# Block means of the value rows in a fused attention and MLP kernel: which operand is stationary in the matmuls that form them

## The chip, the cores and the metric

The kernel runs on one core of one Trainium2 chip. The metric is the device time of one execution in microseconds (us), as a median over runs. One execution was also taken with the hardware profiler, and all rows below are from that one.

## The reference, cut to what matters

Two batches of attention (8 heads, 768 positions, head size 64) feed two MLPs. Each query sees 31 neighbours at most and, beside them, 24 blocks of 32 positions, each standing in with the largest of its keys and the mean of its values:

```python
k_sum = k.reshape(B, H, nb, block, D).max(axis=3)
v_sum = v.reshape(B, H, nb, block, D).mean(axis=3)
...
scores_all = np.concatenate([scores_l_m, scores_s], axis=-1)
scores_all = scores_all - np.max(scores_all, axis=-1, keepdims=True)
a = np.exp(scores_all)
a = a / (np.sum(a, axis=-1, keepdims=True) + 1e-09)
v_all = np.concatenate([v, v_sum], axis=2)
return np.matmul(a, v_all).astype(np.float32)
...
h = x @ w_in
g = np.maximum(h, 0.0) + np.log1p(np.exp(-np.abs(h)))
x = g @ w_out
...
return ((x @ w1) * (x @ w2) @ w3) @ w_out2
```

The change touches only `v_sum`: a 24 x 512 table of means for each of the two batches (512 is 8 heads of 64).

## The kernel before, in words

**Attention.** The 1536 query rows are worked in 12 tiles `u` of 128, six for each batch `b`. Scores: `att_a` (L389, steps `A{u}0`, `A{u}1`) into PSUM pool `px`, tag "x". Softmax: `att_max` on DVE (L400), `att_exp` on ACT (L406), `att_inv` on DVE (L412, L413), `att_norm` on POOL (L418). Then `att_c1` turns the weights by identity matmuls into pool `pa`, tag "a" (L426, steps `T{u}0`, `T{u}1`), DVE and ACT copy them out (L435, L433), and `att_d1` multiplies with the value window `vw` (L447, step `AV{u}`) into pool `ph`, tag "h". Each value window has 96 local rows and, below them in partitions 96 to 119, the 24 means.

**The means.** `v_load` (L340) brings all 768 value rows of a batch into `vt`, 128 rows in each of six groups. `v_sum` (L347, steps `vs{b}s0` and `vs{b}s1`, three groups each) multiplies them with a table of 1/32 and zeros: `sel_t[:, a]` (128 x 24) is the stationary operand, the 512 value columns move, and six float32 matmuls add up in one bank `vs_p`. For tiles 0 and 1 the means go from `vs_p` straight into `vw` (`v0_out`, ACT L357 and DVE L359). For the others ACT copies them to SBUF (`v_keep`, L350), SP stores them to DRAM (`v_store`, L353), and `vw_sum` (L378) loads them into each window. `vs_p` of batch 0 takes a buffer of "x", that of batch 1 one of "a".

**The MLPs.** After the attention come matmuls in three float32r passes each through `mm3` (L239): `H`, `X`, `wm`, `AB`, then the products (L691) and `O`. Weights are loaded by SP (L248) and split by ACT, DVE and POOL (L259 to L283); the first of these lie in the last third of the attention.

**What sets the order.** Nothing is scheduled at run time: class `Order` writes one instruction list. A walk over the PE steps (`pe`, `COST`) gives each a due time, the other engines' steps get theirs backwards from these, and a simulation takes, for each engine, the step with the earliest due time among those that can start within a short look-ahead. Buffers of one tag are handed out strictly in the order of due times: a step whose turn in its tag has not come is not placed, even if a buffer is free. The walk has floors: tile `u` doesn't begin before `16.0 + SP1 * min(u, 8) + SP2 * max(u - 8, 0)`. The PE list goes A0, A1, `vs0s0`, `vs0s1`, then for each `u`: A of tile u+2, at `u == 3` also `vs1s0`, `vs1s1`, then T and AV of tile u. On the chip every engine and the SP queue run their lists strictly in order.

Of the kernel before, what the change touches and what calls it, by code (L numbers as in the profile page):

```python
# [8 lines left out]
F32 = mybir.dt.float32  # L9
# [14 lines left out]
class Order:  # L24
# [21 lines left out]
    def add(self, name, eng, cost, place, fn, needs=(), take=(), give=(), port=False, table=None, lead=0.0):  # L46
        assert name not in self.steps, name
        self.steps[name] = (eng, cost, place, fn, list(dict.fromkeys(d for d in needs if d)), list(take))
        self.extra[name] = (port or eng == "POOL", table, lead)
        for t, b in take:  # L50
            assert b not in self.owner, b
            self.owner[b] = t
        for b in give:
            self.users.setdefault(b, {})[name] = 1
# [150 lines left out]
def fused_kernel(ctx, tc, q, k, kwin, v, vb, w_in, w_out, w1, w2, w3, wo2, mask, sel, ident, out):  # L205
    nc = tc.nc
    P = 128
    B, NT, _, NP, _, _ = q.shape
    S = v.shape[1]
    D = 512  # L210
    NBK = 24
    W = 96
    NK = W + NBK
# [12 lines left out]
    ph = ctx.enter_context(tc.tile_pool(name="ph", bufs=2, space=bass.MemoryType.PSUM))  # L226
    px = ctx.enter_context(tc.tile_pool(name="px", bufs=4, space=bass.MemoryType.PSUM))
    pa = ctx.enter_context(tc.tile_pool(name="pa", bufs=2, space=bass.MemoryType.PSUM))
# [58 lines left out]
    ap_ = att_ctx.enter_context(tc.tile_pool(name="att", bufs=1))  # L287
    mask_t = ap_.tile([P, 3, NK], F32, name="mask_t")
    id_t = ap_.tile([P, P], F32, name="id_t")
    sel_t = ap_.tile([P, 6, NBK], F32, name="sel_t")  # L290
    vs_s = ap_.tile([P, B, D], F32, name="vs_s")

    kt = {}
    kw = {}
# [2 lines left out]
    vw = {}  # L297
# [17 lines left out]
    def kw_copy(t, eng):  # L315
        kw[t] = ap_.tile([P, 2, NP, NK], F32, tag="kw", bufs=3, name="kw")
        for blk in range(2):
            w = wins(t)[blk]
            for h in range(2):
                a, b = max(w, HALF * h), min(w + W, HALF * h + HALF)  # L320
                if a < b:
                    d, s = kw[t][:, blk, :, a - w:b - w], kt[t // NT, h][:, :, a - HALF * h:b - HALF * h]
                    if eng == "ACT":
                        nc.scalar.copy(d, s)
                    else:
                        EN[eng].tensor_copy(d, s)

    def kw_sum(t):
        nc.vector.tensor_copy(
            kw[t][:, :, :, W:NK], ks[t // NT].unsqueeze(1).to_broadcast([P, 2, NP, NBK]))  # L330

    vt = {}
    vs_p = {}

    def v_load(b, i):
        if i == 0:
            vt[b] = xt_p.tile([P, 6, D], F32, tag="xt", name="vt")
        nc.sync.dma_start(vt[b][:, 3 * i:3 * i + 3], v[b, 384 * i:384 * i + 384].rearrange("(a p) c -> p a c", p=P))  # L340

    def v_sum(b, i):
        if i == 0:
            pool, tag = ((px, "x"), (pa, "a"))[b]
            vs_p[b] = pool.tile([P, D], F32, tag=tag, name="vs_p")
        for a in range(3 * i, 3 * i + 3):
            nc.tensor.matmul(vs_p[b][W:NK], sel_t[:, a], vt[b][:, a], start=a == 0, stop=a == 5)  # L347

    def v_keep(b):
        nc.scalar.copy(vs_s[W:NK, b], vs_p[b][W:NK])  # L350

    def v_store(b):
        nc.sync.dma_start(vs_d[b], vs_s[W:NK, b])  # L353
# [8 lines left out]
    def q_load(t):  # L362
        qt[t] = ap_.tile([P, NP, 64, 2], F32, tag="q", bufs=3, name="qt")
        nc.sync.dma_start(qt[t], q[t // NT, t % NT])

    def wins(t):
        j = 2 * (t % NT)
        return [min(max(64 * i - 16, 0), S - W) for i in (j, j + 1)]
# [105 lines left out]
    def step(n):  # L474

        return n // 12, n % 12 // 4, 4 * (n // 12) + n % 4
# [256 lines left out]
    T = B * NT  # L733
# [3 lines left out]
    add = o.add  # L737
# [1 line left out]
    EN = {"POOL": nc.gpsimd, "DVE": nc.vector}  # L739


    COST = {"A": 1.0, "T": .55, "AV": 1.2, "H": 2.72, "X": 1.36, "wm": 2.72, "AB": 2.72, "O": .68, "vs": 1.3, "PR": 1.36}
    at_ = {}
    clock = [8.0]

    def pe(kind, name):
        at_[name] = clock[0]
        clock[0] += COST[kind]

    def tile_a(u):  # L750
        for h in range(2):
            pe("A", f"A{u}{h}")

    def tile_b(u):
        for h in range(2):
            pe("T", f"T{u}{h}")
        pe("AV", f"AV{u}")
# [4 lines left out]
    tile_a(1)  # L762
    for i in range(2):
        pe("vs", f"vs0s{i}")
    for u in range(T):
        clock[0] = max(clock[0], 16.0 + SP1 * min(u, 8) + SP2 * max(u - 8, 0))
        if u + 2 < T:
            tile_a(u + 2)
        if u == 3:
            for i in range(2):  # L770
                pe("vs", f"vs1s{i}")
        tile_b(u)
    pe("H", "H0")
    pe("H", "H4")
# [49 lines left out]
    def padd(kind, name, fn, needs=(), take=(), give=()):  # L824
        add(name, "PE", COST[kind], at_[name], fn, needs, take, give)

# [19 lines left out]
    for b in range(B):  # L846
        for i in range(2):
            add(f"vl{b}{i}", "SP", 3.0, None, lambda b=b, i=i: v_load(b, i), (i and f"vl{b}0",), () if i else [("xt", f"vt{b}")], lead=1)
            padd("vs", f"vs{b}s{i}", lambda b=b, i=i: v_sum(b, i), (f"vl{b}0", f"vl{b}{i}", "sell", i and f"vs{b}s0"),
                 () if i else [("xa"[b], f"vsp{b}")], (f"vt{b}",))  # L850
        add(f"vsc{b}", "ACT", .6, None, lambda b=b: v_keep(b), (f"vs{b}s1",), (), (f"vsp{b}",))
        add(f"vss{b}", "SP", .2, None, lambda b=b: v_store(b), (f"vsc{b}",))


# [27 lines left out]
    for j in jobs:  # L882
        kind, i, p = j
# [14 lines left out]
    for u in range(T):  # L898
        b = u // NT
        eng = "ACT" if u < 2 else "POOL"  # L900
        hs = [h for h in range(2) if wins(u)[0] < HALF * h + HALF and wins(u)[1] + W > HALF * h]
        add(f"kw{u}", eng, 1.3, None, lambda u=u, eng=eng: kw_copy(u, eng),
            [f"kl{2*b+h}" for h in hs], [("kw", f"kw{u}")], [f"kt{2*b+h}" for h in hs])
        add(f"q{u}", "SP", 1.0, -7.5 if u == 0 else None, lambda u=u: q_load(u), (), [("q", f"q{u}")], lead=2)
        add(f"vw{u}", "SP", 1.5, None, lambda u=u: vw_load(u), (), [("g", f"vw{u}")], lead=2)
        add(f"ks{u}", "DVE", .3, None, lambda u=u: kw_sum(u), (f"kw{u}", f"km{2*b+1}"), port=True)
        if u < 2:
            for h in range(2):
                add(f"vs{u}_{h}", "ACT" if h else "DVE", .68, None, lambda u=u, h=h: v0_out(u, h),
                    (f"vw{u}", "vs0s1"), (), ("vsp0",))  # L910
        else:
            add(f"vs{u}", "SP", .27, None, lambda u=u: vw_sum(u), (f"vw{u}", f"vss{b}"), lead=1)
        for h in range(2):
            padd("A", f"A{u}{h}", lambda u=u, h=h: att_a(u, h),
                 (f"ks{u}", f"q{u}", h and f"A{u}0"), [("x", f"sc{u}_{h}")], (f"kw{u}", f"q{u}"))
            for e in range(4 * h, 4 * h + 4):
                add(f"max{u}{e}", "DVE", .205, None, lambda u=u, e=e: att_max(u, e),
                    (f"A{u}{h}", "ml", e and f"max{u}{e-1}"), () if e else [("s", f"s{u}")], (f"sc{u}_{h}",))
                add(f"exp{u}{e}", "ACT", .39, None, lambda u=u, e=e: att_exp(u, e), (f"max{u}{e}",), table="exp")
            add(f"norm{u}{h}", "POOL", 1.0, None, lambda u=u, h=h: att_norm(u, h), (f"inv{u}",), lead=.5)  # L920
            padd("T", f"T{u}{h}", lambda u=u, h=h: att_c1(u, h), (f"norm{u}{h}", "il"),
                 [("a", f"tr{u}{h}")], (f"s{u}",))
            add(f"at{u}{h}", "ACT" if h else "DVE", .66, None, lambda u=u, h=h: att_c2(u, h), (f"T{u}{h}",),
                [("tmp", f"at{u}{h}")], (f"tr{u}{h}",))
        add(f"inv{u}", "DVE", .33, None, lambda u=u: att_inv(u), [f"exp{u}{e}" for e in range(8)])
        padd("AV", f"AV{u}", lambda u=u: att_d1(u),
             (f"at{u}0", f"at{u}1") + ((f"vs{u}_0", f"vs{u}_1") if u < 2 else (f"vs{u}",)),
             [("x" if u >= T - 3 else "h", f"av{u}")], (f"at{u}0", f"at{u}1", f"vw{u}"))
        add(f"xh{u}", "ACT", .6, None, lambda u=u: att_hi(u), (f"AV{u}", u % 4 and f"xh{u-1}"),
            () if u % 4 else [("xt", f"xt{u//4}")])  # L930
        add(f"xl{u}", "DVE", .7, None, lambda u=u: att_lo(u), (f"xh{u}",), (), (f"av{u}",))
# [11 lines left out]
    for n in range(N1):  # L943
        g, c, i = step(n)
# [13 lines left out]
    for s_ in range(12):  # L958
        g, c = divmod(s_, 3)
# [43 lines left out]
    A = lambda *rs: sorted({f"acc{r//3}" for r in rs})  # L1003
# [14 lines left out]
    for i in range(8):  # L1018
# [31 lines left out]
        for c in (1, 2):  # L1050
# [6 lines left out]
            pool = "g" if c == 1 or i == 0 else "b"  # L1057
# [6 lines left out]
    for n in range(N2):  # L1064
        c, i = divmod(n, 8)
# [84 lines left out]
```

## Time and profile before

| | us |
|---|---|
| median of 3 runs | 576.05 (575.16 to 578.75) |
| the profiled execution's own time | 574.96 |
| its span in the trace | 573.2 |

The span is the stretch from the first to the last instruction in the trace; 1.76 us of the profiled execution's time lie around it. PE is TensorE's matmuls, PEld its weight loads, DVE VectorE, ACT ScalarE, POOL GpSimd, SPq the queue of SyncE that issues the DMAs. A float32 matmul of the program stands in the trace as two matmul records with a weight load each, a transpose or a float32r matmul as one; "x12" behind a piece of the chain counts records. The granted clock is TensorE's, as a share of 2.4 GHz.

### The profile page before, as it was taken

What the parts mean: (1) busy time and instruction counts of PE and PEld (TensorE: products, weight loads), DVE (VectorE), ACT (ScalarE), POOL (GpSimd) and SP (SyncE); (2) the same over time, 40 slices, a digit from 0 to 9 for tenths busy, and PEclk for the clock granted to TensorE, in tenths of its full rate; (3) what the DMA queues carried; (4) which work ended last, traced back from release to release, by engine and by line L of the source; (5) the groups of instructions that cost most, each with busy time, mean ns of one, the idle gap of its engine ahead of it and who ended that gap; (6) DMA issues with size and microseconds to landing.
All of it is one profiled execution on the core that took longest, in us unless ns stands there. A gap on an engine that the chain in (4) does not pass through costs nothing.

```text
span 573.2 us, 8418 instructions
## 1 busy us (share of the span) xinstructions
PE 560.9 (98%) x3068; PEld 455.3 (79%) x3068; DVE 401.7 (70%) x786; ACT 322.3 (56%) x688; POOL 156.6 (27%) x143
## 2 busy tenths in 40 slices
PE   8999799999999999999999999999999999999997
PEld 4558678888888888888888888888888888888885
DVE  4668778657787586856586555675777799989710
ACT  4769976667787666665665656566654233222310
POOL 2546543022442342302230333234653000000000
PEclk9999879999999999999999999999999999999999
DMA  8897644143543453423341422225410010000021
GB/s 319 246 273 210 194 122 137 37 111 117 176 132 126 124 170 111 147 73 111 110 119 52 160 74 72 95 93 148 147 37 1 3 73 0 1 0 1 1 93 55
DMA packets 21946, 61.20 MB, mean 107 GB/s; under 512 B 2304, under 2 KB 2688, under 8 KB 21904
## 3 DMA queue, kind: packets, MB, share of 16 engines
q1 hardware_dynamic: 21904, 60.66, 34.3%
q8 instruction: 24, 0.39, 0.3%
q14 instruction: 18, 0.15, 0.1%
HBM read 55.31 MB, written 5.34 MB: 106 GB/s over the span
## 4 chain that ended last, share of the span: by engine, by line
PE 92%; DMA 3%; ACT 2%; DVE 1%; SPq 1%; POOL 0%; issue 0%; POOLq 0%
PE hps L239 23%; PE xps L239 23%; PE abps L691 13%; PE ops L239 11%; PE wps L239 8%; PE abps L239 8%; PE vs_p L347 2%; PE sc L389 2%; PE av L447 2%; DMA sel_t<-in_sel_dram 2%; PE tr L426 1%; DMA raw<-in_w_in_dram 1%; ACT s L406 1%; POOL s L418 0%; DVE vw L359 0%
## 5 line engine op out<-in xcount | busy, mean ns | idle before, releaser
L283 POOL TENSOR_TENSOR w<-cv,w 128x512 fp32r<-128x512 f32 x72 | 96.7, 1347 | 228.8 <-ACT w L279 218.1
L239 PE MATMUL hps<-xt,w 128*128 128x512 f32 x576 | 138.8, 390 | 0.0
L239 PE MATMUL xps<-gt,w 128*128 128x512 f32 x576 | 137.9, 389 | 0.0
L239 PEld LDWEIGHTS hps<-xt,w 128*128 128x128 f32 x576 | 108.4, 188 | 22.6
L239 PEld LDWEIGHTS xps<-gt,w 128*128 128x128 f32 x576 | 108.1, 188 | 22.5
L492 DVE SCALAR_TENSOR_TENSOR tm<-tm,hps 128x512 f32<-128x512 f32 x48 | 33.0, 687 | 59.3 <-ACT tm L489 59.2
L239 PE MATMUL ops<-w,pt 128*128 128x512 f32 x288 | 67.6, 389 | 0.0
L275 DVE SCALAR_TENSOR_TENSOR cv<-cv,raw 128x512 int32<-128x512 int32 x72 | 58.9, 819 | 9.3 <-ACT cv L269 7.4
L489 ACT ACTIVATE tm<-hps 128x512 f32<-128x512 f32 x48 | 28.6, 597 | 62.6 <-PE hps L239 62.6
L239 PEld LDWEIGHTS ops<-w,pt 128*128 128x128 f32 x288 | 54.1, 188 | 11.2
L263 DVE SCALAR_TENSOR_TENSOR raw<-raw 128x512 int32<-128x512 int32 x72 | 57.9, 804 | 4.8 <-ACT raw L259 4.8
L279 ACT CAST w<-cv 128x512 fp32r<-128x512 f32 x72 | 44.4, 619 | 14.2 <-DVE cv L275 9.2
L259 ACT ACTIVATE raw<-raw 128x512 int32<-128x512 uint16 x72 | 48.0, 668 | 1.7 <-DMA raw<-in_w_dram 1.7
L239 PE MATMUL wps<-w 128*128 128x512 f32 x192 | 46.1, 389 | 0.0
L239 PE MATMUL abps<-x2t,w 128*128 128x512 f32 x192 | 44.5, 389 | 0.0
L269 ACT ACTIVATE cv<-raw 128x512 f32<-128x512 f32 x64 | 42.2, 660 | 0.0
L239 PEld LDWEIGHTS abps<-x2t,w 128*128 128x128 f32 x192 | 36.0, 188 | 7.5
L239 PEld LDWEIGHTS wps<-w 128*128 128x128 f32 x192 | 36.0, 188 | 7.5
L498 DVE SCALAR_TENSOR_TENSOR hps<-hps,tm 128x512 f32<-128x512 f32 x48 | 33.5, 697 | 9.7 <-ACT tm L495 7.8
L406 ACT ACTIVATE s<-s,sm 128x120 f32<-128x120 f32 x96 | 36.6, 385 | 5.0 <-DVE sm L400 4.9
L505 DVE TENSOR_TENSOR gt<-hps,gt 128x512 fp32r<-128x512 f32 x48 | 33.0, 688 | 8.8 <-ACT gt L502 7.9
L502 ACT CAST gt<-hps 128x512 fp32r<-128x512 f32 x48 | 28.2, 588 | 15.5 <-DVE hps L498 15.5
(81 smaller groups left out, 689.2 us busy)
## 6 DMA issues: line engine op xcount, KB each, us to landing
raw<-in_w_dram SPq DMA_DIRECT2D x32, 512.0 KB, 3.5
raw<-in_w_in_dram SPq DMA_DIRECT2D x16, 512.0 KB, 3.5
raw<-in_w_out_dram SPq DMA_DIRECT2D x16, 512.0 KB, 3.5
vw<-in_v_dram SPq DMA_DIRECT2D x12, 384.0 KB, 6.5
raw<-in_wo_dram SPq DMA_DIRECT2D x8, 512.0 KB, 3.6
kt<-in_k_dram SPq DMA_DIRECT2D x4, 768.0 KB, 10.3
qt<-in_q_dram SPq DMA_DIRECT2D x12, 256.0 KB, 7.0
vt<-in_v_dram SPq DMA_DIRECT2D x4, 768.0 KB
```

The lines of the kernel that those rows point to most:

```text
L239: nc.tensor.matmul(ps, lhs(a), rhs(b), start=first and i == 0, stop=last and i == 2)
L259: nc.scalar.activation(r[:, :, 0], r.bitcast(U16)[:, :, 1], AF.Copy, bias=-(0.5 - 2.0 ** -14), scale=2.0 ** -13)
L263: nc.vector.scalar_tensor_tensor(r[:, :, 0], r[:, :, 1], -0x80000000, r[:, :, 0], ALU.bitwise_and, ALU.bitwise_or)
L269: nc.scalar.activation(f(c), h, AF.Copy, scale=2.0 ** -112)
L275: nc.vector.scalar_tensor_tensor(c, c, 3, r[:, :, 0], ALU.logical_shift_left, ALU.bitwise_or)
L279: nc.scalar.copy(w[:, 0], f(cvs[kind, i]))
L283: eng.tensor_tensor(w[:, 1], f(cvs[kind, i]), f(w[:, 0]), ALU.subtract)
L406: nc.scalar.activation(s[:, e], s[:, e], AF.Exp, bias=sm[:, 0, e:e + 1], scale=-1.0, accum_out=sm[:, 1, e:e + 1])
L492: nc.vector.scalar_tensor_tensor(tm[n], tm[n], -2.0, hps[n], ALU.mult, ALU.add)
L498: nc.vector.scalar_tensor_tensor(hps[n], hps[n], 0.0, tm[n], ALU.max, ALU.add)
L505: nc.vector.tensor_tensor(gt[n][:, 1], hps[n], f(gt[n][:, 0]), ALU.subtract)
L691: nc.tensor.matmul(ps, w[:, a, (o + kk) * P:(o + kk + 1) * P], rhs(b), start=kk == 0 and n == 0, stop=kk == 1 and n == 2)
```

## The change

`v_sum` takes the values as the stationary operand: for each of the six groups and each of four chunks of 128 columns, `vt[:, a, chunk]` (128 x 128) is loaded as weights and the four columns of `sel_t` that belong to this group move. The result `vs_t` is the table of means turned round (128 columns of the values in the partitions, 4 x 24 in the free dimension), in a buffer of "h". A new ACT step `vsT{b}` copies it to SBUF, and a new PE step `vsu{b}` turns it back into `vs_p` by four matmuls against the identity, which now also wait for the load of `id_t` (step `il`). Everything from `vs_p` on is as before.

```diff
+    vsT = ap_.tile([P, B, 4, NBK], F32, name="vsT")
...
     def v_sum(b, i):
         if i == 0:
-            pool, tag = ((px, "x"), (pa, "a"))[b]
-            vs_p[b] = pool.tile([P, D], F32, tag=tag, name="vs_p")
+            vs_t[b] = ph.tile([P, 4, NBK], F32, tag="h", name="vs_t")
         for a in range(3 * i, 3 * i + 3):
-            nc.tensor.matmul(vs_p[b][W:NK], sel_t[:, a], vt[b][:, a], start=a == 0, stop=a == 5)
+            for c in range(4):
+                nc.tensor.matmul(vs_t[b][:, c, 4 * a:4 * a + 4], vt[b][:, a, c * P:(c + 1) * P],
+                                 sel_t[:, a, 4 * a:4 * a + 4], start=True, stop=True)
+
+    def v_turn(b):
+        nc.scalar.copy(vsT[:, b], vs_t[b])
+
+    def v_back(b):
+        pool, tag = ((px, "x"), (pa, "a"))[b]
+        vs_p[b] = pool.tile([P, D], F32, tag=tag, name="vs_p")
+        for c in range(4):
+            nc.tensor.matmul(vs_p[b][W:NK, c * P:(c + 1) * P], vsT[:, b, c], id_t, start=True, stop=True)
...
-    COST = {"A": 1.0, "T": .55, "AV": 1.2, "H": 2.72, "X": 1.36, "wm": 2.72, "AB": 2.72, "O": .68, "vs": 1.3, "PR": 1.36}
+    COST = {"A": 1.0, "T": .55, "AV": 1.2, "H": 2.72, "X": 1.36, "wm": 2.72, "AB": 2.72, "O": .68, "vs": 1.2, "vsu": .55, "PR": 1.36}
...
         pe("vs", f"vs0s{i}")
+    pe("vsu", "vsu0")
...
                 pe("vs", f"vs1s{i}")
+            pe("vsu", "vsu1")
...
-                 () if i else [("xa"[b], f"vsp{b}")], (f"vt{b}",))
-        add(f"vsc{b}", "ACT", .6, None, lambda b=b: v_keep(b), (f"vs{b}s1",), (), (f"vsp{b}",))
+                 () if i else [("h", f"vst{b}")], (f"vt{b}",))
+        add(f"vsT{b}", "ACT", .3, None, lambda b=b: v_turn(b), (f"vs{b}s0", f"vs{b}s1"), (), (f"vst{b}",))
+        padd("vsu", f"vsu{b}", lambda b=b: v_back(b), (f"vsT{b}", "il"), [("xa"[b], f"vsp{b}")])
+        add(f"vsc{b}", "ACT", .6, None, lambda b=b: v_keep(b), (f"vsu{b}",), (), (f"vsp{b}",))
...
-                    (f"vw{u}", "vs0s1"), (), ("vsp0",))
+                    (f"vw{u}", "vsu0"), (), ("vsp0",))
```

## Rows read from the trace of the kernel before

**Rows 1.** Page, part 1: busy us, share of the span and instructions by engine.

```profile
PE 560.9 (98%) x3068; PEld 455.3 (79%) x3068; DVE 401.7 (70%) x786; ACT 322.3 (56%) x688; POOL 156.6 (27%) x143
```

**Rows 2.** Windows: us, busy of PE, PEld, DVE, ACT, POOL, granted clock, DMA share, GB/s.

```profile
110.00:376.00 266.00, 266.00 (x1175) 220.28 (x1174) 181.47 (x266) 172.47 (x300) 77.94 (x58) 1.00 0.36 113
```

**Rows 3.** The chain that ended last, in order of time: start, us, what.

```profile
13.53 5.32 PE vs_p L347 x12
...
18.87 0.59 ACT vw L357
...
23.80 1.15 PE av L447 x32
...
31.81 1.08 PE av L447 x32
...
33.86 5.27 PE vs_p L347 x12
39.16 0.59 ACT vs_s L350
39.74 0.14 issue
...
48.41 1.02 PE tr L426 x8
...
52.50 0.35 SPq L364
...
54.17 7.29 DMA raw<-in_w_in_dram
61.48 0.43 DVE cv L271
...
62.87 6.17 ACT s L406 x32
...
73.90 1.98 PE av L447 x32
75.88 1.89 PE tr L426 x8
...
82.01 8.43 PE hps L239 x36
...
569.38 0.69 DVE osb L725
```

**Rows 4.** Weight loads by line: duration ns min/median/max; the last from part 5: mean.

```profile
L347 PEld LDWEIGHTS vs_p<-vt,sel_t x24: 98/103/103, 13.5 to 38.1; 128*24 128x24 f32 x24
...
L447 PEld LDWEIGHTS av<-at,vw x384: 132/138/232, 23.8 to 81.7; 120*64 120x64 f32 x192
...
L426 PEld LDWEIGHTS tr<-id_t,s x96: 133/138/223, 20.6 to 77.1; 128*120 128x120 f32 x96
...
L239 PEld LDWEIGHTS hps<-xt,w 128*128 128x128 f32 x576 | 108.4, 188 | 22.6
```

**Rows 5.** Page, part 5: ACT's exponentials; busy us, mean ns, idle before.

```profile
L406 ACT ACTIVATE s<-s,sm 128x120 f32<-128x120 f32 x96 | 36.6, 385 | 5.0 <-DVE sm L400 4.9
```

**Rows 6.** SP's waits up to 82 us: total us, times, longest.

```profile
SPq L353 <- ACT vs_s L350: 6.3, 1, 6.3
```

**Rows 7.** Windows of the attention, columns as in rows 2.

```profile
22.00:24.00 2.00, 0.82 (x20) 0.60 (x16) 1.97 (x15) 2.00 (x10) 0.00 (x0) 1.00 0.52 150
...
40.00:42.00 2.00, 1.23 (x14) 0.85 (x15) 0.94 (x4) 1.71 (x8) 0.00 (x0) 1.00 1.08 239
...
64.00:66.00 2.00, 1.31 (x18) 0.88 (x14) 1.79 (x18) 2.00 (x13) 1.66 (x2) 1.00 1.00 289
66.00:68.00 2.00, 0.68 (x5) 0.41 (x4) 1.42 (x10) 2.00 (x11) 0.36 (x2) 1.00 0.46 178
68.00:70.00 2.00, 1.57 (x24) 1.39 (x26) 1.20 (x3) 2.00 (x9) 1.84 (x2) 0.55 0.00 0
...
78.00:80.00 2.00, 2.00 (x9) 1.64 (x8) 1.50 (x3) 1.93 (x4) 1.01 (x1) 0.89 0.65 240
```

More of the change, by code (lines that the diff above doesn't have):

```diff
@@ L334, in fused_kernel @@
     vt = {}
+    vs_t = {}
     vs_p = {}
```

## The prediction

> **What bounds the kernel now.** I began with the page's busy shares: PE is busy for 560.9 of 573.2 us [rows 1], so a saving elsewhere counts only where PE waits for it. The windows then show where PE is the limit for certain: from 110 to 376 us it has no idle at all [rows 2], and in the chain of waits every piece from 82.01 us to the last copy out at 569.38 is PE's [rows 3]. Everything from there on costs the same in both kernels, so the change counts by how much it moves the end of the attention, which now hands over at about 82 us.
>
> The chain of that part, in order of time [rows 3], is where the reader should look next. Both batches' means stand on it: 5.32 us at 13.53 and 5.27 us at 33.86. Behind the first come the copies by ACT and DVE into the first two windows, then PE is the chain from 23.80 to 52.50, with the second batch's means inside. At 52.50 it passes to the SP queue, to a load of weights (7.29 us to landing), to DVE, which stands at L271 until that load is in at 61.48, to the last exponentials on ACT (6.17 us), to POOL, and back to PE. So a change of PE's time before 52.50 shifts the rest, but the rest has its own sources, the transfers above all.
>
> **The matmuls of the means.** Before, a batch takes 12 records of 512 moving columns, 5.32/12 = 443 ns each [rows 3]; the weight load (24 columns) hides behind them. After, it takes 6 groups x 4 chunks = 24 matmuls, 48 records, each with a load of 128 columns, and 4 columns moving. The moving side is next to nothing: what paces a record is now the load, which no long matmul hides.
>
> No row has such a stream, so I bound it. The durations of loads grow with their columns: 98 to 103 ns for 24, 132 to 138 for 64, 188 for 128 [rows 4]. From 24 to 128 columns that is about 87 ns for 104 columns, 0.84 ns a column, so 107 ns for 128, and some 80 ns that don't depend on the columns. Whether those 80 overlap is told by `av`: 32 records in 1.08 us [rows 3] are 34 ns each over two halves of the array, so 68 ns per half, though each load lasts 138 ns. The fixed part overlaps, and 68 ns are the 64 columns (54) and 14 more. For 128 columns I get 107 to 121 ns and take 115: 48 x 0.115 = **5.5 us a batch, against 5.3 before. The swap itself gains nothing.** The bounds: at best 34 ns a record, the pace of `av` (1.6 us); at worst 188 ns, a load that overlaps with nothing (9.0 us). I stay near the `av` and L239 rows because these are the loads of plain matmuls; the one row against my slope, 120 columns in 138 ns at L426 [rows 4], is of transposes.
>
> The Trainium skill ("TensorE: Matmul & The Clock Gate", "LDWEIGHTS (loading the stationary operand)") gives a load as its columns over 1.2 GHz, however many rows it has. By that alone 128 columns take 107 ns and a batch an estimated 5.1 us; the slope of rows 4 agrees with it.
>
> **What is added.** The ACT copy of 128 x 96 out of PSUM: between nothing (if hidden) and the 0.59 us of a copy of 512 columns [rows 3]; nearest is the exponential of 128 x 120, 0.385 us [rows 5]. Around it stand handovers of 0.03 us (39.13 to 39.16) and 0.14 us, as around L350 [rows 3]. Together 0.55 us in which PE waits. It can fill little of it: `vsu` comes ahead of the next scores (batch 0, tag "x") and the next transposes (batch 1, tag "a") in the strict order of buffers, so these can't pass it; only T0 could in batch 0. Queued behind the waiting `vsu` on PE are A2, T0 and A3, or T3 and AV3; ACT's exponentials stand behind `vsT`, but ACT is waiting for `vs_p` there today (the L357 and L350 copies), so they lose nothing more.
>
> Turning back is 4 float32 matmuls of 128 moving columns, 8 records. The nearest row is `tr`: 8 records of 128 columns in 1.02 us [rows 3]. I take 1.0; a bound below is 8 x 34 ns = 0.3, above 8 x 188 ns = 1.5.
>
> So per batch 5.5 + 0.55 + 1.0 = 7.1 us from the first record to the finished `vs_p`, against 5.3: **1.8 us later for batch 0, and 1.8 for batch 1**, 3.6 in all. Of smaller things I count none: "x" and "a" buffers are held shorter, "h" is held for the means instead (its AV at that place has been copied out by then); `id_t` is wanted a few us sooner but is issued right beside the window loads; the new due times are 0.35 us later per batch (2 x 1.2 + 0.55 for 2 x 1.3) and the floor of tile 8 (16 + 8 x 5 = 56) swallows that, so no due time of the MLPs moves. If the simulation still swaps steps, that is worth a us or two either way.
>
> **How much reaches the end.** Batch 0's 1.8 us pass whole to AV0 at 23.80 [rows 3]: PE has only A2, T0 and A3 to do and waits already (busy for 0.82 of the 2 us from 22 us [rows 7]). They reach the SP queue too: it stands 6.3 us at the store L353 until ACT has made `vs_s`, with batch 1's keys and values behind it [rows 6]; the transfers run at only 0.52 just after [rows 7]. Batch 1's 1.8 us lengthen a stretch in which PE is the chain. Against that, DVE stands until 61.48 for a weight load whose issue hangs on the SP queue but whose 7.29 us go through busy transfers [rows 3]; thinner traffic makes them shorter. I pass three quarters: 3.6 x 0.75 = 2.7 us (bounds: the 1.8 of one batch, the whole 3.6). The profiled execution took 574.96 us and would take 577.7. It lies 1.09 us under the median of the runs, so for the median I say 576.05 + 2.7 = **578.7 us**, slower by 0.5%.
>
> **Rivals.**
>
> *The loads overlap well and the means get short.* At 34 ns a record a batch takes 1.6 + 0.55 + 1.0 = 3.2 us, 2.1 less than before; two batches, three quarters of it: 3.2 us faster, 572.9. It decides from the pace at which the swap breaks even: (5.3 - 1.55)/48 = 78 ns a record. For it: `av` really runs at that pace. Against it: there two loads of 64 columns go to two halves of the array, here one of 128 fills it. The Trainium skill ("TensorEngine Tiling", "Instruction Overhead") speaks for it: each matmul has some 60 cycles of overhead, and one with a single moving column costs as one with 60. By that, 48 records of 60 cycles at 2.4 GHz are an estimated 1.2 us a batch; no row here shows a full load at such a pace. Chance 0.18.
>
> *The clock falls.* The granted clock is 1.00 up to 68 us, 0.55 in the window from 68 and back near 79 [rows 7]. Before it fell, PE was busy for 1.31 and 0.68 of 2 us, much of it transposes. What the change puts in place of 512-column matmuls streams 4 columns per load for some 5 us, then PE waits for ACT. If the chip counts this as little, the clock falls to 1.2 GHz there. The price: `av` goes from 1.08 to 1.98 us for 32 records, `tr` from 1.02 to 1.89 for 8 [rows 3]. A stretch like that of rows 7, 10 us long, costs up to 5 us, and some 3 where PE has slack; twice 3 on top of 2.7 is 8.7 us: 584.8. Against it: the loads keep coming every 115 ns, and the stretch from 40 to 42 us, where PE is busy for 1.23 of 2 us, keeps 1.00 [rows 7]. Chance 0.18.
>
> *The loads don't overlap.* At 188 ns a batch takes 9.0 + 1.55 = 10.6 us, 5.3 more; two batches, three quarters to the whole: 8 to 10.5 us, 585. For it: the durations of rows 4; against it: `av`. Chance 0.10.
>
> *It is hidden or reshuffled.* The transfers and the written order decide the end and PE's time doesn't show: 576, give or take 2. Chance 0.10. That the change doesn't act at all is excluded by the diff: the 24 long records go.
>
> **How the numbers follow.** The forecast has 0.44, with its own range 576.5 to 580.5. For 8 in 10 I take in all but the tails: 573.8 below, which leaves out most of the rival at 34 ns, and 586 above, which holds the clock and most of the loads. A measurement of this kernel tells about 1% (5.8 us) from no change. Slower by more than that are the clock and the loads that don't overlap, 0.28, less what of them stays small: 0.23. Faster by more would take both batches at 34 ns and a lucky order behind them: 0.04. Within 1%: 0.73.
>
> **What would show it.** In the changed profile: 96 loads of 128 columns at L347's successor with starts some 115 ns apart (34 to 78 means the first rival, about 190 the third); 16 records turning back at about 125 ns; a PE wait for ACT of about half a us ahead of them; the copies into the first windows at about 20.6 instead of 18.87; AV0 at 25.6; a granted clock of 1.00 until the last softmax; the dense `hps` stretch from about 84.7 instead of 82.01, and unchanged pieces behind it. Wrong would be: a fall of the clock between 15 and 45 us, the last exponentials not later than now, or PE idle after 85 us.

## The result and the profile after

The changed kernel takes 582.12 us (median of 9 runs, 579.35 to 584.69) against 576.05: 1.0105 times as long, with a 95% interval of 1.0082 to 1.0128. It is 6.1 us slower; 2.7 were forecast. The profiled execution took 582.12 us with a span of 580.3, 7.1 us more than before.

The page first: busy shares as in [rows 1], and the row of the granted clock in 40 slices of 14.5 us, in tenths, where 9 stands for 90% or more.

```profile
PE 569.6 (98%) x3156; PEld 470.2 (81%) x3156; DVE 400.7 (69%) x786; ACT 322.5 (56%) x690; POOL 156.0 (27%) x143
...
PEclk9798969999999999999999999999999999999999
```

PE is busy for 8.7 us more. The clock row has a 7 in its second slice and an 8 in its fourth, in the stretches of the two batches' means; the 6 in the sixth slice is the end of the softmax, which the kernel before has too. Windows of the changed kernel show it closer (columns as in rows 2):

```profile
14.00:16.00 2.00, 2.00 (x20) 2.00 (x19) 1.78 (x17) 1.60 (x9) 1.64 (x2) 1.00 1.07 243
16.00:18.00 2.00, 2.00 (x18) 2.00 (x18) 0.40 (x3) 1.53 (x9) 1.18 (x3) 0.89 1.04 284
18.00:20.00 2.00, 2.00 (x11) 2.00 (x11) 0.10 (x1) 0.00 (x0) 1.88 (x2) 0.50 1.08 261
...
24.00:26.00 2.00, 2.00 (x28) 1.67 (x26) 1.32 (x7) 1.11 (x2) 0.49 (x2) 0.90 0.00 0
...
40.00:42.00 2.00, 2.00 (x18) 2.00 (x17) 1.79 (x2) 0.00 (x0) 0.35 (x2) 0.87 1.08 214
42.00:44.00 2.00, 2.00 (x11) 2.00 (x11) 0.23 (x1) 0.00 (x0) 0.00 (x0) 0.50 1.06 216
...
48.00:50.00 2.00, 2.00 (x34) 1.67 (x34) 0.87 (x2) 1.39 (x7) 0.00 (x1) 0.93 0.68 160
...
74.00:76.00 2.00, 1.71 (x24) 1.29 (x22) 0.74 (x2) 2.00 (x13) 2.00 (x3) 0.90 0.58 156
...
84.00:86.00 2.00, 2.00 (x8) 1.72 (x7) 1.96 (x3) 1.17 (x3) 0.00 (x0) 0.54 0.75 252
```

A mean of 0.89 over the window from 16 us is 1.56 us at full clock and 0.44 at half, so the clock fell at 17.6 us; by the same working it came back at 24.4, fell again at 41.5 and came back at 48.3. PE stands as busy without a gap in both windows in which it fell, so the busy share alone would not have shown the fall. From the window of 14 us to that of 18 us the records in it go from 20 to 11. What this did to the work stands in the chain of waits, to be laid beside [rows 3]:

```profile
13.40 6.57 PE vs_t L349 x48
19.97 0.95 PE tr L438 x4
20.91 1.85 PE vs_p L359 x8
22.76 0.02 issue
22.78 0.59 ACT vw L369
...
27.42 1.15 PE av L459 x32
...
37.84 7.00 PE vs_t L349 x48
44.84 0.02 issue
44.86 0.25 ACT vsT L353
45.11 0.04 issue
45.15 1.90 PE vs_p L359 x8
...
84.79 3.29 PE hps L239 x12
...
89.17 8.39 PE hps L239 x36
```

The streams take 6.57 and 7.00 us instead of 5.32 and 5.27, turning back 1.85 and 1.90. The copies into the first windows begin at 22.78 instead of 18.87, the first `av` at 27.42 instead of 23.80, and the dense `hps` stretch at 89.17 instead of 82.01: 7.16 us later, which is the whole difference of the spans. The loads' own row, with durations in ns (min/median/max), answers to [rows 4]; a load lasts 192 ns, but 48 of them fit into 6.57 us, so they overlap:

```profile
L349 PEld LDWEIGHTS vs_t<-sel_t,vt x96: 186/192/338, 13.4 to 44.4; 128*128 128x128 f32 x96
```

### The profile page after: what moved, and what is told of

Same layout as the page of the kernel before. It is cut to its first block, busy times and chain, and to the rows that moved or that the text cites. A ratio compares the mean times of both kernels' runs of the same rounds, so it can differ in the third digit from the quotient of the medians.

```text
span 580.3 us, 8594 instructions
## 1 busy us (share of the span) xinstructions
PE 569.6 (98%) x3156; PEld 470.2 (81%) x3156; DVE 400.7 (69%) x786; ACT 322.5 (56%) x690; POOL 156.0 (27%) x143
## 4 chain that ended last, share of the span: by engine, by line
PE 94%; ACT 2%; DMA 1%; DVE 1%; SPq 1%; issue 0%; DVEq 0%
PE hps L239 23%; PE xps L239 22%; PE abps L703 13%; PE ops L239 11%; PE abps L239 7%; PE wps L239 7%; PE vs_t L349 2%; PE av L459 2%; PE sc L401 2%; PE tr L438 2%; DMA sel_t<-in_sel_dram 1%; ACT s L418 1%; PE vs_p L359 1%; DVE s L412 0%; DVE at L447 0%; DVE ks L311 0%
```

## The experiments

All figures are ratios to the kernel before, run on the same chip beside each kernel, with 95% intervals. The theory: the loss is the clock. The main rivals: the added copy, wait and turn; the reshuffled list.

**Keeping the clock with the same instructions (`wide_moving`).**

```diff
-                nc.tensor.matmul(vs_t[b][:, c, 4 * a:4 * a + 4], vt[b][:, a, c * P:(c + 1) * P],
-                                 sel_t[:, a, 4 * a:4 * a + 4], start=True, stop=True)
+                k = 4 * (4 * a + c)
+                nc.tensor.matmul(vs_t[b][:, k:k + 96], vt[b][:, a, c * P:(c + 1) * P],
+                                 sel_t[:, a, 4 * a:4 * a + 4].unsqueeze(1).to_broadcast([P, 24, 4]), start=True, stop=True)
```

> Edit: the changed kernel, but each of the 96 records of the means moves its four selecting columns 24 times over (96 columns, by a repeating access pattern); the copies behind the first land in PSUM columns that the next matmul writes anew, so the result is the same. Instructions, waits and the written order are those of the changed kernel. Theory (clock: the stream of 4-column matmuls lets TensorE's clock fall to 1.2 GHz some 4 us into each batch, and the loads at half speed, the turning back and the next steps pay for it): the granted clock stays 1.00 from 10 to 60 us, a stream takes 48 x 0.111 = 5.3 us instead of 6.6 and 7.0, turning back 1.0 us instead of 1.9, the dense H stretch begins at 84 to 85.5 us instead of 89.2, and the time is 1.003 to 1.006 of before (577.5 to 579.5 us). Rival 1 (the added copy, wait and turn, with the reshuffled list, cost it all): still about 1.0105 of before, since none of these is touched. Rival 2 (the chip counts loads and not moving columns, so the clock falls all the same): about 1.0105 or above, with the clock at 0.50 near 18 and 42 us.

Measured: 577.08 us, 1.0011 (0.9999 to 1.0024). Two windows where the changed kernel stood at half clock, the two in which the later fall begins and ends, and the chain:

```profile
18.00:20.00 2.00, 2.00 (x20) 1.80 (x19) 0.25 (x2) 0.24 (x1) 1.73 (x2) 1.00 1.05 292
...
42.00:44.00 2.00, 1.82 (x16) 1.22 (x15) 1.08 (x4) 1.07 (x3) 1.56 (x2) 1.00 1.06 236
...
74.00:76.00 2.00, 1.01 (x7) 0.46 (x5) 1.97 (x4) 1.97 (x4) 0.52 (x1) 0.76 0.00 0
...
80.00:82.00 2.00, 2.00 (x7) 1.61 (x6) 1.51 (x4) 1.64 (x4) 0.46 (x1) 0.54 0.66 250
```

```profile
13.57 5.57 PE vs_t L350 x48
...
19.57 1.00 PE vs_p L361 x8
...
35.66 5.54 PE vs_t L350 x48
...
41.52 1.07 PE vs_p L361 x8
...
84.92 8.39 PE hps L239 x36
```

The clock holds at 1.00 through both batches, the streams take 5.6 and 5.5 us and the turn 1.0. Nothing was removed; 92 more columns were moved per record, and 1.0105 became 1.0011, below the 1.003 to 1.006 of the theory. In both traces every engine works the same instructions on the same tiles in the same order. So the 0.0094, or 5.4 us, are the price of the two falls with all that follows from them (the later half-clock stretch too is shorter here, 75.0 to 81.8 us against 75.6 to 85.8). Rivals 1 and 2 both fall here.

**The added steps alone (`turn_alone`).**

```diff
-            for c in range(4):
-                nc.tensor.matmul(vs_t[b][:, c, 4 * a:4 * a + 4], vt[b][:, a, c * P:(c + 1) * P],
-                                 sel_t[:, a, 4 * a:4 * a + 4], start=True, stop=True)
+            nc.tensor.matmul(vs_t[b][W:NK], sel_t[:, a], vt[b][:, a], start=a == 0, stop=a == 5)
...
-        nc.scalar.copy(vsT[:, b], vs_t[b])
+        nc.scalar.copy(vsT[W:NK, b], vs_t[b][W:NK, 0:96].rearrange("p (c n) -> p c n", c=4))
...
+    for b in range(B):
+        nc.gpsimd.memset(vsT[:, b], 0.0)
```

> Edit: the changed kernel with the old sums put back into its first step (selecting table stationary, 512 value columns moving), and copy and turning back kept as a load of the same size on some of these sums; the table of means that the windows get is therefore not the means. Measures the added copy, waits, turn and the reshuffled list without the narrow stream. Theory (clock): the clock stays 1.00, each batch is longer by the copy with its handovers (0.3 us) and the turn (1.0 us), 2.6 us in all of which some 90% reach the end: 1.003 to 1.006 of before. Rival 1 (these added steps and the list are the whole loss): about 1.0105. Rival 2 (they are hidden): 1.000.

Measured: 578.05 us, 1.0029 (1.0009 to 1.0049). The dense `hps` stretch begins at 83.97, 2.0 us later than before, and the clock is 1.00 until 70 us, so copy, wait and turn don't make it fall. With the changed kernel's order they cost 1.7 us over the runs, not the loss. (The copy takes 24 partitions and 96 columns instead of 128 and 96, and POOL clears the rest of `vsT` at the start.)

**One batch at a time (`batch0_alone`, `batch1_alone`).** The edit is a condition on `b` in `v_sum` and in the three steps behind it, with the old form for the other batch:

```diff
+        if b != 0:
...
+            return
```

> Edit: the change for batch 0 alone, batch 1 summed as before. Theory (clock, each batch pays on its own): one fall of the clock near 17.5 us, the second batch at 1.00; the copies into the first windows at 22.8 us as in the changed kernel; 3.9 us later there, 90% of it at the end: 1.005 to 1.007 of before. Rival (the delay of batch 0 is taken up by slack before the second batch): 1.000 to 1.002.

> Edit: the change for batch 1 alone, batch 0 summed as before. Theory (clock, each batch pays on its own): one fall of the clock some 4 us into the stream that begins near 34 us; 3.9 us later there, 90% of it at the end: 1.005 to 1.007 of before. Rival (only the start of the attention matters, since transfers bound the middle): 1.000 to 1.002.

Measured: 580.76 us, 1.0082 (1.0056 to 1.0108) for batch 0, and 577.43 us, 1.0024 (1.0010 to 1.0039) for batch 1. The two add up to 1.0106, as large as the whole loss, but neither ratio is in the 1.005 to 1.007 that was expected: batch 0's lies above it and batch 1's below. Batch 0 alone goes as foreseen up to the windows (one fall near 18 us, the copies at 22.92, 1.00 in the second batch). The chain and the windows of batch 1 alone:

```profile
33.83 8.36 PE vs_t L356 x48
...
42.51 1.90 PE vs_p L366 x8
```

```profile
34.00:36.00 2.00, 2.00 (x20) 2.00 (x20) 1.89 (x15) 1.98 (x9) 1.93 (x2) 0.99 1.07 237
36.00:38.00 2.00, 2.00 (x12) 2.00 (x11) 1.95 (x5) 0.00 (x0) 1.41 (x2) 0.50 1.09 234
...
76.00:78.00 2.00, 1.46 (x12) 0.92 (x9) 1.19 (x2) 1.98 (x3) 2.00 (x3) 0.73 0.10 39
78.00:80.00 2.00, 2.00 (x10) 1.90 (x9) 1.97 (x3) 1.56 (x4) 2.00 (x2) 0.50 0.00 0
80.00:82.00 2.00, 2.00 (x9) 1.61 (x9) 1.87 (x3) 1.71 (x4) 0.71 (x2) 0.91 0.17 29
```

Here the clock fell just before 36 us, so the stream took 8.36 us and PE ended the turn at 44.41 instead of 39.13: 5.3 us later, more than the 3.9 expected. Yet over the runs only 1.4 reach the end. (In the profiled execution it is 3.8, a span of 577.0 against 573.2, but that is the second slowest of its twelve.) Its last half-clock stretch is much shorter (76.9 to 80.4, against 68.2 to 78.4 before, worked out from the means in rows 7 and here). And the end of its attention is in another order than before: the transposes of the last tiles come in a row of 12 records, as in `due_alone` below, a list that by itself gains 2.1 us. The timelines of batch 1 alone and of `due_alone`:

```profile
76.61 2.90 PE L445 MATMUL tr<-id_t,s 128*120 128x128 f32 x12 [0.45 <-POOL s L437]
```

```profile
72.35 3.01 PE L426 MATMUL tr<-id_t,s 128*120 128x128 f32 x12 [0.32 <-POOL s L418]
```

That these two pay the rest back is argued, not shown.

**New due times alone (`due_alone`).**

```diff
-    COST = {..., "vs": 1.3, "PR": 1.36}
+    COST = {..., "vs": 1.475, "PR": 1.36}
```

> Edit: the kernel before, with the planned cost of one half of the means raised from 1.3 to 1.475, so that the walk stands where the changed kernel's walk stands after each batch (2 x 1.475 = 2 x 1.2 + 0.55). No instruction is added or taken away. Theory (the clock and the added steps make the loss, not new due times): 0.998 to 1.002 of before, the granted clock at 1.00 until the last softmax. Rival (a small shift of due times reshuffles the list at the price of some us): 1.004 or more.

Measured: 574.03 us, 0.9964 (0.9950 to 0.9978). A miss, and the rival's mechanism with the other sign: the same instructions in another order are 2.1 us faster. Its last half-clock stretch is shorter too (granted clock 0.997 over the span against 0.991). So the list moves the time by as much as the steps do, and the next two runs set the changed kernel's walk back.

**The change with the old due times (`changed_old_due`), and without the falls (`wide_old_due`).**

```diff
-    COST = {..., "vs": 1.2, "vsu": .55, "PR": 1.36}
+    COST = {..., "vs": 1.025, "vsu": .55, "PR": 1.36}
```

> Edit: the changed kernel with the planned cost of half a batch of means lowered from 1.2 to 1.025, so that the walk stands after each batch where that of the kernel before stands (2 x 1.025 + 0.55 = 2 x 1.3). What is open: raising the same cost in the kernel before, with nothing else, made it 0.9964 of before, so a shift of the walk is worth 2 us either way, and may hide part of the price of the added steps. Theory (the list of the changed kernel carries a gain of some 2 us of that kind): slower than the changed kernel by about 2 us, 1.012 to 1.015 of before. Rival (with the added steps the list differs anyway and the walk's 0.35 us mean nothing): 1.009 to 1.012, as the changed kernel.

> Edit: wide_moving (each record of the means moves its four columns 24 times over) with the planned cost of 1.025 of changed_old_due. Tells the three parts of the loss apart: new due times, added steps, clock. Theory (the parts add: the clock is worth 0.0094 of before under either list, the new due times hide some 0.006): changed_old_due 1.0165 less 0.0094, so 1.006 to 1.008 of before, with the clock at 1.00 until the last softmax. Rival (under this list the loss is of another kind than the clock): 1.012 or more with the clock at 1.00. Rival 2 (the clock is worth the whole, and the old list costs nothing without a fall): 1.001.

Measured: 585.88 us, 1.0165 (1.0147 to 1.0182), and 581.24 us, 1.0095 (1.0065 to 1.0125). The first is above both ranges that were named for it. By these figures the new due times were hiding 0.0060 of the change's price; that may be too much, since the four runs with the old ones (granted clock 0.974 to 0.980) are about 2 us, or 0.003, slower than those five of the changed kernel's nine that had a like clock. Waits between 40 and 95 us show a place where the lists differ (total us, times, longest), first with the old due times, then in the changed kernel:

```profile
DVE cv L271 <- DMA raw<-in_w_in_dram: 4.6, 1, 4.6
...
PE av L459 <- DVE at L447: 5.8, 5, 3.4
```

```profile
DVE cv L271 <- DMA raw<-in_w_in_dram: 1.9, 1, 1.9
...
PE av L459 <- DVE at L447: 0.9, 2, 0.8
```

With the old due times DVE stands 4.6 us in front of a weight load, with the copies behind it that `av` waits for. The clock is worth 0.0070 under this list (1.0165 less 1.0095) and 0.0094 under the other: of the expected size, not quite equal, and 1.0095 lies between the theory's 1.006 to 1.008 and the rival's 1.012. With the clock at 1.00 until the last softmax, the added steps and the order that they bring cost 5.5 us under the old walk, twice the forecast.

**The clock's price by itself (`warm_tail`, `wide_and_warm`).**

```diff
+    def fill(ps, n):
+        idb = id_t.bitcast(BF16)
+        for k in range(n):
+            nc.tensor.matmul(ps[:, 0:2] if k % 2 else ps[:, 2:4], idb[:, 0:P], idb, start=True, stop=True)
...
+        if t in (9, 10):
+            fill(tr, 6)
...
+        if t == 9:
+            fill(o, 10)
```

> Edit: the kernel before, with 34 bfloat16 matmuls (two bit views of the identity, 256 columns moving, results overwritten by what follows) in places where PE waits at the end of the attention: 6 ahead of each of the four groups of transposes of tiles 9 and 10, 10 ahead of the value matmuls of tile 9. Tests the price of the clock by itself, on the fall that the kernel before already has at 68 to 79 us. Theory (half clock in a stretch where PE is on the chain costs about half of what it lasts): the clock stays at 1.00 there, PE's pieces from 69 to 78 us take half as long, and the time is 0.995 to 0.998 of before. Rival (in this stretch ACT and POOL end last and the clock is idle talk): 1.000, or above where a filler is longer than the wait that it fills.

> Edit: wide_moving with the 34 fillers of warm_tail at the end of the attention, so that the changed kernel's structure runs without any fall of the clock. Theory (a half-clock stretch costs its share wherever it lies, and wide_moving has one left at 75 to 81 us): clock 1.00 over the span, and as much below wide_moving as warm_tail is below before in proportion to the stretch (7 us against 10): 0.997 to 0.999 of before. Rival (the end of this list is bound by ACT and POOL): 1.001.

Measured: 574.06 us, 0.9964 (0.9950 to 0.9978), and 575.05 us, 0.9983 (0.9968 to 0.9998). In `warm_tail` the window that had 0.55 in [rows 7] reads:

```profile
68.00:70.00 2.00, 2.00 (x21) 1.87 (x20) 1.01 (x10) 2.00 (x13) 0.70 (x1) 1.00 0.66 225
```

Added work on the bounding engine makes the kernel 2.1 us faster, because a stretch of 10 us at half clock goes away. That is the price of a fall in a kernel without the change, with the written order of all its other work as it was. With all falls gone, the changed structure (0.9983) and the old one (0.9964) differ by about 1 us; the two intervals overlap.

**PE's time for batch 1 (`strips_batch1`, `strips_pool`).**

```diff
+            if b:
+                g = 32 * (a % 4)
+                nc.tensor.matmul(vs_p[b][g:g + 32], sel2_t[:, a], vt[b][:, a], start=a < 4, stop=a > 1)
+                continue
...
+            for a in range(6):
+                g = 32 * (a % 4) + 4 * (a // 4)
+                nc.sync.dma_start(vs_d[b][4 * a:4 * a + 4], vs_s[g:g + 4, b])
```

> Edit: the kernel before, but the six groups of batch 1 write to four column strips of the array in turn (partitions 0, 32, 64, 96; a second selecting table of 32 columns for it), so that the last record of one group and the first of the next can run side by side, and the valid rows are stored by six small DMAs instead of one. Tests whether PE's time for the means of batch 1 reaches the end at all: the clock theory says that this stretch is PE's chain. Theory: 12 records in some 7 slots of 443 ns, 3.1 us instead of 5.3, and 0.996 to 0.999 of before. Rival (batch 1's means are covered by transfers, so only the clock and not PE's time counts here): 1.000, or 1.001 to 1.002 with the five more DMAs on SP's queue.

> Edit: as strips_batch1, but the second selecting table is made by POOL from the first (one memset, six small copies) instead of being loaded, since in strips_batch1 PE waited 1.9 us ahead of the means of batch 1 at the place where that late load was the new condition. Theory (that load caused the wait, and PE's time for batch 1 is on the path): the means begin by 34 us and take 1.9 us, PE runs on, 0.995 to 0.999 of before. Rival (the transfers of batch 1's values gate this place, so nothing is won): 1.000 to 1.005, with PE waiting there as before.

Measured: 578.49 us, 1.0049 (1.0031 to 1.0066), and 575.35 us, 0.9981 (0.9965 to 0.9997). PE's timeline of the first and of the second, with the wait ahead in brackets:

```profile
35.78 1.91 PE L350 MATMUL vs_p<-vt,sel_t 128*32 128x512 f32 x12 [1.94 <-issue]
```

```profile
34.09 1.91 PE L350 MATMUL vs_p<-vt,sel_t 128*32 128x512 f32 x12
```

The first is slower than both of its ranges. Loading a second table made PE wait 1.94 us; made on the chip, the wait is gone. The means then take 1.9 us instead of 5.3, but only 1.1 us reach the end. The gain is still there at the next `av`, which begins at 38.99 instead of 41.89. In the profiled execution it is lost near 60 us, where PE stands for a copy on DVE, behind a transfer of MLP weights that lands at 62.33; the one in the chain of the kernel before landed at 61.46 (7.29 us from 54.17, [rows 3]). A piece of the chain, PE's timeline and two windows there:

```profile
51.31 11.02 DMA raw<-in_w_in_dram
```

```profile
63.43 1.94 PE L460 MATMUL av<-at,vw 120*64 120x64 f32 x32 [3.91 <-DVE at L448]
```

```profile
62.00:64.00 2.00, 0.57 (x12) 0.57 (x14) 1.65 (x9) 0.39 (x2) 0.00 (x0) 0.88 1.10 239
...
66.00:68.00 2.00, 2.00 (x20) 1.64 (x16) 0.84 (x9) 0.52 (x3) 1.01 (x2) 0.77 0.62 219
```

Behind this wait the clock is at half for 3.4 us (63.5 to 66.9), a fall that the kernel before doesn't have. So the time is in the theory's range, but most of what PE saves for batch 1 goes to a wait for a transfer, as the rival had it of an earlier place.

**The best version (`due_and_warm`)** joins the edits of `due_alone` and `warm_tail`.

> Edit: the two faster kernels together: the kernel before with the planned cost of 1.475 of due_alone and the fillers of warm_tail. If the list of due_alone wins by other means than the clock at the end of the attention, the gains add up: 0.993 to 0.994 of before, clock 1.00. If it wins because its half-clock stretch is shorter (its granted clock is 0.993 to 0.997 over the span against 0.991), they overlap: 0.995 to 0.997.

Measured: 572.35 us, 0.9931 (0.9914 to 0.9949), granted clock 0.999 in the profiled run. The gains add up, so by the rule stated beforehand the list of `due_alone` wins by something else than the clock; what, stays open. It is faster than both kernels and has neither the swap nor the turn.

## Why the prediction was right or wrong

**The step that failed is the clock, which the sum held at 1.00.** The forecast of 2.7 us added up the streams, the copy, the wait and the turn at full clock, put the fall at nothing, and left it to a rival with a chance of 0.18. It fell in both batches, for 6.8 us each time. `wide_moving` puts the price at 5.4 us (4.0 under the old due times), more than the whole forecast. The two reasons against the fall, that "the loads keep coming every 115 ns" and that 40 to 42 us keeps 1.00 with PE partly idle, don't carry: the clock fell under an unbroken stream of loads. The rival's price was good: "twice 3" us.

**With the clock held, the forecast's chain comes out.** In the profiled execution of `wide_moving` the first table of means is finished at 20.57 instead of 18.85 (1.7 us later; 1.8 forecast), the second at 42.59 instead of 39.13 (3.5; 3.6 forecast), and the dense `hps` stretch begins at 84.92 (84.7 forecast). These are single executions, though, one 1.1 us under the median of its kernel and the other 0.8 us over: over the runs the added steps cost 0.6 us under this list, less than forecast.

**Right: the swap itself gains nothing.** Batch 0's stream ran 4.16 us at full clock and 2.41 at half, which counts for 1.2: 5.4 us for 48 records, 112 ns each (batch 1: 111), against 115 forecast. The rivals at 34 and at 188 ns are both excluded. The Trainium skill ("TensorE: Matmul & The Clock Gate", "LDWEIGHTS (loading the stationary operand)") had 107 ns, which agrees within 5%. The Trainium skill's 60 cycles a matmul ("TensorEngine Tiling", "Instruction Overhead") would have been an estimated 25 ns, and the measurement decides against taking that as the pace where every matmul has a load of its own.

**Right in kind: copy, wait, turn.** The copy took 0.25 us instead of 0.385. The turn took 1.0 at full clock, as forecast (`wide_moving`), and 1.85 to 1.90 in the changed kernel. In batch 0 T0 alone filled the wait, as said, and the first half of it was enough; it is the 0.95 us piece in the chain.

**Not settled: how much reaches the end.** In the profiled executions PE came out of the second turn at 47.05 instead of 39.13, 7.9 us later, and the dense stretch began 7.16 us later: 90%, not 75%. But the kernel before was profiled in an execution 1.09 us under its median; against the 6.1 us between the medians it is 77%.

**Wrong: the list.** "The floor of tile 8 swallows that" is true of the due times of the MLPs, but the order inside the attention was worth 0.0036 to 0.0084 (three pairs of runs that differ in this cost alone), at or above the "us or two" that I allowed. In this change it happened to help, which is luck, and so the sum of the added steps looked smaller (1.0011 for all of `wide_moving`) than it is under the old walk.

**Signs named beforehand:** the wait for ACT ahead of the turn came in batch 1, the fall of the clock between 15 and 45 us was listed as what would prove the forecast wrong, and PE has no idle past the hand-over.

## What to carry to other kernels

Making the streamed operand narrow leaves the weight loads as the pace, so price the loads before counting columns, from a slope over rows of several widths. Then read the granted clock beside the busy share: a stretch of many loads and few columns looked 100% busy and still lost the clock, and of each fall's 6.8 us half or more lay on the work behind it. Where an order is planned from estimated costs, run one kernel in which only the estimate moves, since a change of 0.35 us in the plan was worth 2 to 5 us here.

## What the runs showed of the hardware that was not expected

- A load of 128 float32 columns with 4 columns moving paces at 111 to 112 ns at 2.4 GHz and slows with the clock: in `batch1_alone`, 2.1 us at full clock hold some 19 records, and the other 29 took 6.2 us, 215 ns each.
- Moving 96 columns instead of 4 behind each of these loads costs next to nothing (5.57 us for 48 records, 116 ns each) and the clock held.
- Six float32 matmuls of 512 columns over four column strips took 1.91 us for their 12 records, 159 ns each against 443: more overlap than the pairs that were expected.
- In the changed kernel's 9 runs the mean granted clock and the time go together: five at 0.977 to 0.979 took 582.1 to 584.7 us, four at 0.985 to 0.988 took 579.4 to 581.8. So the time spent at half clock differs from run to run.
